# Second attention: an exponential left as two bf16 tiles that TensorE adds

## The chip, the cores and the metric

The kernel runs on one core of a Trainium2 chip. The metric is the device time of one execution in microseconds (us), lower is better. Engines: TensorE (PE) multiplies matrices into PSUM, ScalarE (ACT) computes functions, VectorE (DVE) does elementwise work, GpSimd (POOL) hardly takes part here, SyncE (SP) starts nearly all transfers.

## The reference

Four blocks in a row, each added to x: a linear attention A, a softmax attention B, and both again. The change is in the second B:

```python
def _B_ref(x, wqkv, wo):            # x: 1 x 2048 x 1024 after a layernorm, bf16; H = 32 heads, Dh = 32
    qkv = (x @ wqkv).reshape(B, S, 3, H, Dh).transpose(2, 0, 3, 1, 4)
    q, k, v = qkv[0], qkv[1], qkv[2]
    scores = jnp.einsum("bhqd,bhkd->bhqk", q, k) * (Dh ** -0.5)
    p = _softmax(scores, axis=-1)
    o = jnp.einsum("bhqk,bhkd->bhqd", p, v)
    return o.transpose(0, 2, 1, 3).reshape(B, S, D) @ wo

x = x + _A_ref(_layernorm(x), A_wqkv, A_w_phi, A_wo)
x = x + _B_ref(_layernorm(x), B_wqkv, B_wo)
x = x + _A_ref(_layernorm(x), A_wqkv, A_w_phi, A_wo)
x = x + _B_ref(_layernorm(x), B_wqkv, B_wo)
```

Nothing is subtracted from the scores before the exponential; numerator and denominator come from the same exponentials.

## The kernel before

**The planner.** The program is not written in the order in which it runs. Each step is an entry with an engine, an estimated duration, the steps it needs, the buffers it holds and a priority. On the host, `Sched.run` plays these entries through in estimated time (line 183 on) and so fixes the order on every engine. The chip then runs these fixed orders, held together by semaphores. An estimate that changes can therefore change the order. Estimates that matter here: an activation of n elements n/1200 + 0.064 us; a VectorE step of n elements n/960 + 0.15, and half of the per-element part for a `tensor_scalar` from SBUF to SBUF; one accumulation step of four matmuls 0.225.

**The attention.** There are 32 turns per attention (4 chunks of 512 queries by 8 groups of four heads). A turn has two passes, and each pass 8 blocks of 128 keys with 4 units: 64 units a turn, 2048 in an attention. A unit is one score tile of 128 keys by 512 queries for one head. `score` (L1082) writes it to PSUM with a 32-row matmul. A group of three units goes to ACT as one exponential of 1536 columns (L1139), in two PSUM areas by turns (banks 0 to 2 and 3 to 5). The accumulation (L1264) takes two units in one step: four matmuls of 32 columns each, for each unit one with the values and one with ones, so that numerator and denominator grow together in bank 6.

**The second path.** Some units go past ACT. `spare` picks one that stands 36 to 44 units ahead in the list. It comes either as a fourth score in bank 7 (`attach`, when that bank is free) or in place of the third of a group, whose exponential then has 1024 columns (at most once in some four groups, `MIX`). Two such units make a pair. `convert` (L1221) adds an offset to each score tile in PSUM and leaves it as an integer in one of two `work` slots ("xy"): read as a float, it has the power of two in its exponent bits and the fraction in its mantissa. When the pair is full, `exp_dve` runs five steps over both units (1024 columns): mantissa with exponent zero into the slot "xx", of which there is one (L1048); exponent alone, in place (L1051); and three multiply-adds (all recorded at L1046) that multiply the factors of a polynomial by the power of two and leave a bf16 tile E1 in the arena. A new pair is opened only if a slot of each kind, a turn's allowance (`MOST`) and little waiting work on DVE (`LOAD`) allow it.

**Around it.** PE also runs the projections that later turns and the output need, through bank 7 (L507). Where PE was busy less than 75% of the last 3.4 us, the planner adds filler matmuls: on `onesD` (recorded at L507) or on `zero` (L1490). The two attentions have the same code; the second runs from about 1558 to 2388 us. The arena is 162 KB per partition and handed out by the planner; an E1 tile holds 2 KB, and six may live.

Of the kernel before, what the change touches and what calls it, by code (L numbers as in the profile page):

```python
# [11 lines left out]
ALU = mybir.AluOpType  # L12
AX = mybir.AxisListType
BF16 = mybir.dt.bfloat16
F32 = mybir.dt.float32
I32 = mybir.dt.int32

EPS_LN = 1e-5
EPS_DEN = 1e-6
DH = 32  # L20
C512 = 512
# [316 lines left out]
MIX = (lambda i: 4, lambda i: 3)  # L338
# [20 lines left out]
def kernel(  # L359
# [644 lines left out]
    def b_last(c, t, fc, prio, w, oT, banks, eng, part=None, lo=0, hi=4):  # L1004
# [22 lines left out]
        else:  # L1027
# [2 lines left out]
        dma(prio, lambda: nc.sync.dma_start(  # L1030
            out=out[0, xs, fc * C512:(fc + 1) * C512], in_=r_v()), [e], [r_b], kb=128)

    def exp_dve(pair, prio):


        n = len(pair["got"])
        y_b, e_b = pair["bufs"]
        x_b, x = fixed("xx", [(10,)])
        sch.enter(x_b, prio)
        y_v, x_v, e_v = (lambda v=v: v()[:, 0:n, :] for v in (pair["y"], x, pair["e"]))  # L1040

        def ts(fn, deps, bufs):
            return sch.later("DVE", n * 512 / 1920 + 0.15, fn, deps, bufs, prio)

        def stt(out_, in0, scalar, in1, dep, bufs):
            return sch.later("DVE", dve_us(n * 512), lambda: nc.vector.scalar_tensor_tensor(  # L1046
                out=out_(), in0=in0(), scalar=scalar, in1=in1(), op0=ALU.add, op1=ALU.mult), [dep], bufs, prio)
        m = ts(lambda: nc.vector.tensor_scalar(  # L1048
            out=x_v().bitcast(I32), in0=y_v().bitcast(I32), scalar1=0x007FFFFF, scalar2=0x3F800000,
            op0=ALU.bitwise_and, op1=ALU.bitwise_or), pair["got"], [y_b, x_b])  # L1050
        a = ts(lambda: nc.vector.tensor_scalar(  # L1051
            out=y_v().bitcast(I32), in0=y_v().bitcast(I32), scalar1=0x7F800000, scalar2=None,
            op0=ALU.bitwise_and), [m], [y_b])
# [4 lines left out]
    def attention(base, kT, vT, q_of, gate, most, mix, turns, pos):  # L1058


        units = [
# [93 lines left out]
        def close(pair):  # L1155
            if pair is not None:
                last = pair["units"][0]
                eo = exp_dve(pair, prio_of(last) - LEAD)
                for b in pair["bufs"]:
                    b.left -= 1  # L1160
                for k, u in enumerate(pair["units"]):
                    used(u, eo, pair["bufs"][1], pair["flat"], k)
                state["pair"] = None

        def wants(prio):
# [19 lines left out]
        def spare(rows, turn, more):  # L1185

            pair = state["pair"]
            if state["at"] + AHEAD + 8 > len(units) or (pair is None and (state["turn"].get(turn, 0) + 2 > most(turn) or sch.load("DVE") > LOAD)):
                return None
            u = next((u for u in units[state["at"] + AHEAD:state["at"] + AHEAD + 8]  # L1190
                      if u[4] in rows and u not in taken
                      and all(d.done == 2 for d in needs(u))), None)
            if u is None:
                return None
            new = list(more)
            if pair is None:
                y_b, y_v = fixed("xy", [(8,), (9,)])
                e_b, e_v = sb("E1", 2, C512)
                new += [y_b, e_b]
            for b in new:  # L1200
                sch.enter(b, prio_of(u) - LEAD)
            if not sch._alloc(new):
                for b in new:
                    sch.queue[b.cls][0].remove(b)
                return None
            if pair is None:
                state["pair"] = {"got": [], "units": [], "y": y_v, "e": e_v, "bufs": (y_b, e_b),
                                 "flat": lambda: e_v().rearrange("p a b -> p (a b)")}
                for b in (y_b, e_b):
                    b.left += 1  # L1210
            taken.add(u)
            return u

        def convert(so, u, s_b, s_v, turn):

            pair = state["pair"]
            y_b, y_v = pair["bufs"][0], pair["y"]
            k = len(pair["got"])
            so.bufs += holds(u)
            pair["units"].append(u)  # L1220
            pair["got"].append(sch.later("DVE", dve_us(512), lambda: nc.vector.tensor_scalar(  # L1221
                out=y_v().bitcast(I32)[:, k, :], in0=s_v(), scalar1=EXP2_OFF * ONE, scalar2=0.0,
                op0=ALU.add, op1=ALU.max), [so], [s_b, y_b], prio_of(u) - LEAD, None, True))
            state["turn"][turn] = state["turn"].get(turn, 0) + 1
            if k:
                close(pair)
# [16 lines left out]
        if True:  # L1243
            for qc, g in turns:
                T = []
                end = (qc, g) == turns[-1]
                for pp in range(2):
                    a_b, a_v = ps("acc", [(6,)])
                    last = None
                    for d in range(8):  # L1250
                        prio = base + 10 * pos[(qc, g)] + 5 * pp + 0.5 * d
                        for u in range(2):
                            us = [(qc, g, pp, d, 2 * u + k) for k in range(2)]
                            kc = 4 * (d // 2) + 2 * u + d % 2
                            v_b, v_v, v_done = vT[(g // 4, kc // 4)]

                            def fn(us=us, kc=kc, u=u, d=d, a_v=a_v, v_v=v_v, g=g, pp=pp):
                                for k in range(2):
                                    eb, ev, x = e_of[us[k]]
                                    j = 2 * pp + k  # L1260
                                    for what in range(2):
                                        col = 64 * ((pp + what) % 2) + 32 * k
                                        o = (g % 4) * P + j * DH
                                        nc.tensor.matmul(  # L1264
                                            out=a_v()[col:col + 32, :],
                                            lhsT=v_v()[:, kc % 4, o:o + DH] if what == 0 else ones_bf[:],
                                            rhs=ev()[:, x * C512:(x + 1) * C512],
                                            start=(d == 0 and u == 0), stop=(d == 7 and u == 1),
                                            tile_position=(0, col), skip_group_check=True)
# [81 lines left out]
    for layer in range(2):  # L1351
# [70 lines left out]
        for g in range(G):  # L1422
            pr = at + 10 * pos[(0, g)]
            w = slab("w2", pr - 11, B_w[:, :, g * P:(g + 1) * P], P) if g else wq0
            for qc in range(NC):
# [8 lines left out]
        oTs = attention(at, kT, vT, q_of, gate, MOST[layer], MIX[layer], turns, pos)  # L1434
# [91 lines left out]
```

## Time and profile before

| What | before |
|---|---|
| median of 3 runs | 2403.58 us (2401.06 to 2406.6) |
| profiled execution, its own time | 2402.28 us |
| its span, first to last instruction | 2400.5 us |
| mean granted TensorE clock | 0.993 |
| units converted by DVE, whole program (L1221) | 302 |

The span is the profile's; the time of an execution has 1.8 us around it. PE is TensorE's matmuls, PEld its weight loads, and "busy" of PE includes the modelled tail of each matmul. In a group of instructions the figures behind the bar are the busy time in us and the mean duration of one in ns, then the engine's idle time in front of the group and what ended it. A wait is written "waiting engine and line <- what ended the wait: us in total, times, longest".

### The profile page before, as it was taken

What the parts mean: (1) busy time and instruction counts of PE and PEld (TensorE: products, weight loads), DVE (VectorE), ACT (ScalarE), POOL (GpSimd) and SP (SyncE); (2) the same over time, 40 slices, a digit from 0 to 9 for tenths busy, and PEclk for the clock granted to TensorE, in tenths of its full rate; (3) what the DMA queues carried; (4) which work ended last, traced back from release to release, by engine and by line L of the source; (5) the groups of instructions that cost most, each with busy time, mean ns of one, the idle gap of its engine ahead of it and who ended that gap; (6) DMA issues with size and microseconds to landing.
All of it is one profiled execution on the core that took longest, in us unless ns stands there. A gap on an engine that the chain in (4) does not pass through costs nothing.

```text
span 2400.5 us, 61762 instructions
## 1 busy us (share of the span) xinstructions
PE 2248.0 (94%) x26839; PEld 864.3 (36%) x26904; DVE 1861.2 (78%) x2540; ACT 2042.4 (85%) x1893; POOL 28.0 (1%) x72
## 2 busy tenths in 40 slices
PE   7999999999999998999998999899999999999998
PEld 4443443333333333333333444333333333333333
DVE  6997763565668788987996776456699999998997
ACT  6325657999999999999997456499999999999998
POOL 0000000000000000000000000000000000000000
PEclk9999999999999999999999999899999999999999
DMA  9020010112222221113314100000111111021110
GB/s 220 14 75 1 5 36 17 41 37 48 51 59 73 82 59 55 54 48 110 117 36 143 36 5 25 18 24 26 37 30 41 33 31 33 25 61 42 42 31 28
DMA packets 205192, 117.03 MB, mean 49 GB/s; under 512 B 125304, under 2 KB 194936, under 8 KB 204152
## 3 DMA queue, kind: packets, MB, share of 16 engines
q1 hardware_dynamic: 203864, 110.98, 17.1%
q8 instruction: 210, 3.44, 0.6%
q10 hardware_dynamic: 1056, 2.10, 0.3%
q14 instruction: 62, 0.51, 0.1%
HBM read 77.40 MB, written 15.19 MB: 39 GB/s over the span
## 4 chain that ended last, share of the span: by engine, by line
ACT 35%; PE 13%; issue 9%; DVE 4%; DMA 1%; ACTq 0%; SPq 0%; DVEq 0%
ACT arena L1139 33%; PE psum L503 6%; PE psum L507 2%; PE psum L1082 2%; PE psum L1264 1%; DVE arena L598 1%; ACT arena L696 1%; DVE arena L594 0%; DMA arena<-rd 0%; PE psum L872 0%; DMA arena<-arena 0%; DVE arena L700 0%; PE psum L817 0%; DVE work L1046 0%; DVE arena L709 0%
## 5 line engine op out<-in xcount | busy, mean ns | idle before, releaser
L1139 ACT ACTIVATE arena<-psum 128x1536 bf16<-128x1536 f32 (+1 forms) x1338 | 1712.4, 1553 | 43.0 <-PE psum L1082 38.6
L1264 PE MATMUL psum<-arena 128*32 128x512 bf16 x4096 | 621.1, 383 | 1.5 <-DVE arena L1279 1.4
L1264 PE MATMUL psum<-arena,ones_bf 128*32 128x512 bf16 x4096 | 621.3, 383 | 0.0
L507 PE MATMUL psum<-arena 128*32 128x512 bf16 (+1 forms) x8768 | 607.4, 377 | 12.4 <-DVE xT L1001 2.9
L1082 PE MATMUL psum<-arena 32*128 32x512 bf16 x4096 | 526.5, 383 | 79.2 <-ACT arena L1139 72.7
L503 PE MATMUL psum<-arena 128*128 128x512 bf16 (+1 forms) x1976 | 457.8, 377 | 24.6 <-DVE arena L598 6.0
L1082 PEld LDWEIGHTS <-arena 32*128 32x128 bf16 x4096 | 178.1, 91 | 605.0 <-issue 594.3
L1046 DVE SCALAR_TENSOR_TENSOR work<-work 128x1024 f32<-128x1024 f32 (+1 forms) x310 | 369.4, 1191 | 6.0
L507 PEld LDWEIGHTS <-arena 128*32 128x32 bf16 x8768 | 195.7, 95 | 258.3 <-issue 153.3
L503 PEld LDWEIGHTS <-arena 128*128 128x128 bf16 x2032 | 194.0, 99 | 259.2 <-issue 54.8
L1221 DVE TENSOR_SCALAR work<-psum 128x512 int32<-128x512 f32 x302 | 207.6, 687 | 93.9 <-PE psum L1082 91.2
L1264 PEld LDWEIGHTS <-arena 128*32 128x32 bf16 x4096 | 169.9, 95 | 210.4 <-issue 149.0
L1046 DVE SCALAR_TENSOR_TENSOR arena<-work 128x1024 bf16<-128x1024 f32 (+1 forms) x155 | 184.5, 1190 | 2.6
L1264 PEld LDWEIGHTS <-ones_bf 128*32 128x32 bf16 x4096 | 168.5, 95 | 29.1 <-issue 3.6
L931 DVE CAST arena<-psum 128x512 bf16<-128x512 f32 (+1 forms) x128 | 83.6, 653 | 110.4 <-PE psum L507 110.2
L696 ACT ACTIVATE arena<-psum 128x512 bf16<-128x512 f32 x80 | 42.8, 599 | 85.2 <-PE psum L503 53.8
L1051 DVE TENSOR_SCALAR work<-work 128x1024 int32<-128x1024 int32 (+1 forms) x155 | 104.7, 676 | 3.9
L1048 DVE TENSOR_SCALAR work<-work 128x1024 int32<-128x1024 int32 (+1 forms) x155 | 104.3, 673 | 3.6
L834 ACT ACTIVATE arena<-psum 128x512 bf16<-128x512 f32 x128 | 69.8, 597 | 40.9 <-PE psum L503 32.4
L594 DVE TENSOR_TENSOR arena<-xT,arena 128x1024 f32<-128x1024 bf16 x64 | 78.0, 1220 | 32.3 <-ACT arena L581 32.2
L1279 DVE COPY arena<-psum 128x512 f32<-128x512 f32 x126 | 86.3, 685 | 14.2 <-PE psum L1264 13.2
L507 PE MATMUL psum<-xT,onesD 128*32 128x512 bf16 x1200 | 91.3, 380 | 1.5 <-DVE arena L931 0.6
(97 smaller groups left out, 1387.6 us busy)
## 6 DMA issues: line engine op xcount, KB each, us to landing
arena<-rd SPq DMA_DIRECT2D x62, 256.0 KB
arena<-in_A_wqkv_dram SPq DMA_DIRECT2D x10, 1024.0 KB
arena<-in_B_wqkv_dram SPq DMA_DIRECT2D x35, 256.0 KB
arena<-arena SPq DMA_DIRECT2D x256, 32.0 KB
arena<-in_B_wo_dram SPq DMA_DIRECT2D x32, 256.0 KB
arena<-wd_k SPq DMA_DIRECT2D x8, 1024.0 KB
arena<-arena SPq DMA_DIRECT2D x80, 64.0 KB
arena<-in_A_wo_dram SPq DMA_DIRECT2D x4, 1024.0 KB
```

Of the source, the lines that this page charges most:

```text
L503: nc.tensor.matmul(out_, lhsT=lhsT, rhs=rhs, start=start, stop=stop, skip_group_check=True)
L507: nc.tensor.matmul(out_[ks, :], lhsT=lhsT[:, ks], rhs=rhs, start=start, stop=stop, tile_position=(0, 32 * k), skip_group_check=True)
L594: s1 = op("DVE", dve_us(1024), lambda pr=pr, w_v=w_v: nc.vector.tensor_tensor(out=w_v(), in0=xT[:, pr, csl(c)], in1=m_v().unsqueeze(1).to_ ...
L931: return soon(op("DVE", dve_us(n), lambda: nc.vector.tensor_copy(out=dst(), in_=src()), [dep], bufs, prio))
L1046: return sch.later("DVE", dve_us(n * 512), lambda: nc.vector.scalar_tensor_tensor(out=out_(), in0=in0(), scalar=scalar, in1=in1(), op0=ALU ...
L1048: m = ts(lambda: nc.vector.tensor_scalar(out=x_v().bitcast(I32), in0=y_v().bitcast(I32), scalar1=0x007FFFFF, scalar2=0x3F800000, op0=ALU.b ...
L1051: a = ts(lambda: nc.vector.tensor_scalar(out=y_v().bitcast(I32), in0=y_v().bitcast(I32), scalar1=0x7F800000, scalar2=None, op0=ALU.bitwise ...
L1082: nc.tensor.matmul(out=out_, lhsT=kT[g][1]()[r, pp, d * P:(d + 1) * P], rhs=q_of[(qc, g)][1]()[r, (pp + j // 2) % 2, :], start=True, stop= ...
L1139: ex = make("ACT", act_us(w * C512), lambda: nc.scalar.activation(out=e_v()[:, 0:w * C512], in_=s_v()[:, 0:w * C512], func=ACT.Exp, scale= ...
L1221: pair["got"].append(sch.later("DVE", dve_us(512), lambda: nc.vector.tensor_scalar(out=y_v().bitcast(I32)[:, k, :], in0=s_v(), scalar1=EXP ...
L1264: nc.tensor.matmul(out=a_v()[col:col + 32, :], lhsT=v_v()[:, kc % 4, o:o + DH] if what == 0 else ones_bf[:], rhs=ev()[:, x * C512:(x + 1) ...
L1279: cp = op("DVE", dve_us(512), lambda t_v=t_v, a_v=a_v: nc.vector.tensor_copy(out=t_v(), in_=a_v()), [last], [a_b, t_b], prio - 4)
```

## The change

In the second attention alone (`SPLIT = (False, True)`), a pair's exponential is left as a sum of two bf16 tiles. The first is again polynomial times power of two. The second is the power of two times a fixed 7-bit mantissa (0x39), made exactly by masking the high half of the integer and setting these mantissa bits. PE adds the two when it accumulates. With the constant term taken out, the polynomial needs two multiply-adds where it needed three:

| step | before, 1024 columns | after |
|---|---|---|
| 1 | mantissa to xx, int32 | the same, other exponent bits |
| 2 | exponent alone, int32, in place in xy | exponent and fixed mantissa, uint16, every second half-word of xy into the second half of E1 |
| 3 | (xx + R) * xy into xy | gone |
| 4 | (xx + B) * xx into xx | (xx + B') * xx into xx |
| 5 | (xx + C) * xy into E1, bf16 | (xx + C') * xy into the first half of E1, bf16 |

The tile E1 has room for four tiles of 512 columns in place of two. In the accumulation each converted unit brings two more matmuls, which come behind the four of its step; the planner's estimate of that step grows by 0.2165 us, once per step.

```diff
+EXP2S_OFF = 125.32242318458253
+EXP2S_B, EXP2S_C = -0.05462324649185644, 1.5306572635884585
+EXP2S_D = 0x0039
+SPLIT = (False, True)
...
+    def high(v):
+        return v.bitcast(U16).rearrange("p a (b t) -> p a b t", t=2)[:, :, :, 1]
...
+        if pair["split"]:
+            e2_v = lambda: pair["e"]()[:, 2:2 + n, :]
+            m = ts(lambda: nc.vector.tensor_scalar(
+                out=x_v().bitcast(I32), in0=y_v().bitcast(I32), scalar1=0x007FFFFF, scalar2=0x3F000000,
+                op0=ALU.bitwise_and, op1=ALU.bitwise_or), pair["got"], [y_b, x_b])
+            a = ts(lambda: nc.vector.tensor_scalar(
+                out=e2_v().bitcast(U16), in0=high(y_v()), scalar1=0x7F80, scalar2=EXP2S_D,
+                op0=ALU.bitwise_and, op1=ALU.bitwise_or), [m], [y_b, e_b])
+            h = stt(x_v, x_v, EXP2S_B, x_v, a, [x_b])
+            return stt(e_v, x_v, EXP2S_C, y_v, h, [x_b, y_b, e_b])
...
-        def used(u, ex, e_b, e_v, x):
-            e_of[u] = (e_b, e_v, x)
+        def used(u, ex, e_b, e_v, x, xs=None):
+            e_of[u] = (e_b, e_v, (x,) if xs is None else (x, xs))
             av = av_of[u]
+            if xs is not None:
+                if not any(len(e_of[o][2]) > 1 for o in units[index[u] - u[4] % 2:index[u] - u[4] % 2 + 2] if o != u and o in e_of):
+                    av.dur += 0.2165
...
-                e_b, e_v = sb("E1", 2, C512)
+                e_b, e_v = sb("E1", 4 if split else 2, C512)
...
-                                for k in range(2):
-                                    eb, ev, x = e_of[us[k]]
-                                    j = 2 * pp + k
-                                    for what in range(2):
+                                for n in range(2):
+                                    for k in range(2):
+                                        eb, ev, xs = e_of[us[k]]
+                                        if n >= len(xs):
+                                            continue
+                                        x = xs[n]
+                                        j = 2 * pp + k
+                                        for what in range(2):
...
+                                                start=(d == 0 and u == 0 and n == 0),
+                                                stop=(d == 7 and u == 1 and n == len(xs) - 1),
```

More of the change, by code (lines that the diff above doesn't have):

```diff
@@ L16 @@
 I32 = mybir.dt.int32
+U16 = mybir.dt.uint16
 EPS_LN = 1e-5
@@ L1056, in exp_dve, with attention @@
         return stt(e_v, x_v, EXP2_C, y_v, h, [x_b, y_b, e_b])
-    def attention(base, kT, vT, q_of, gate, most, mix, turns, pos):
+    def attention(base, kT, vT, q_of, gate, most, mix, turns, pos, split):
         units = [
@@ L1161, in close @@
                 for k, u in enumerate(pair["units"]):
-                    used(u, eo, pair["bufs"][1], pair["flat"], k)
+                    used(u, eo, pair["bufs"][1], pair["flat"], k, 2 + k if split else None)
                 state["pair"] = None
@@ L1206, in spare @@
             if pair is None:
-                state["pair"] = {"got": [], "units": [], "y": y_v, "e": e_v, "bufs": (y_b, e_b),
+                state["pair"] = {"split": split, "got": [], "units": [], "y": y_v, "e": e_v, "bufs": (y_b, e_b),
                                  "flat": lambda: e_v().rearrange("p a b -> p (a b)")}
@@ L1221, in convert @@
             pair["got"].append(sch.later("DVE", dve_us(512), lambda: nc.vector.tensor_scalar(
-                out=y_v().bitcast(I32)[:, k, :], in0=s_v(), scalar1=EXP2_OFF * ONE, scalar2=0.0,
+                out=y_v().bitcast(I32)[:, k, :], in0=s_v(), scalar1=(EXP2S_OFF if split else EXP2_OFF) * ONE, scalar2=0.0,
                 op0=ALU.add, op1=ALU.max), [so], [s_b, y_b], prio_of(u) - LEAD, None, True))
@@ L1257, in fn @@
                             def fn(us=us, kc=kc, u=u, d=d, a_v=a_v, v_v=v_v, g=g, pp=pp):
-                                for k in range(2):
-                                    eb, ev, x = e_of[us[k]]
-                                    j = 2 * pp + k
-                                    for what in range(2):
[L1262 to L1269, printed above, removed]
+                                for n in range(2):
[6 more added lines that the diff above has]
+                                        for what in range(2):
+                                            col = 64 * ((pp + what) % 2) + 32 * k
+                                            o = (g % 4) * P + j * DH
+                                            nc.tensor.matmul(
+                                                out=a_v()[col:col + 32, :],
+                                                lhsT=v_v()[:, kc % 4, o:o + DH] if what == 0 else ones_bf[:],
+                                                rhs=ev()[:, x * C512:(x + 1) * C512],
+                                                start=(d == 0 and u == 0 and n == 0),
+                                                stop=(d == 7 and u == 1 and n == len(xs) - 1),
+                                                tile_position=(0, col), skip_group_check=True)
                             last = op("PE", 0.225, fn, flat([last, v_done[(kc % 4, g % 4 // 2)]]),
@@ L1433 @@
                     q_of[(qc, g)] = q_back(g, qc, at + 10 * pos[(qc, g)] - 12, away)
-        oTs = attention(at, kT, vT, q_of, gate, MOST[layer], MIX[layer], turns, pos)
+        oTs = attention(at, kT, vT, q_of, gate, MOST[layer], MIX[layer], turns, pos, SPLIT[layer])
         if last:
```

## The prediction

> **What bounds the kernel now.** I read the page's totals first, then the stages of the second attention (1558 to 2388 us, the only part that the diff reaches), then the instructions and waits inside them.
>
> ```profile
> span 2400.5 us, 61762 instructions
> PE 2248.0 (94%) x26839; PEld 864.3 (36%) x26904; DVE 1861.2 (78%) x2540; ACT 2042.4 (85%) x1893; POOL 28.0 (1%) x72
> ```
>
> By these shares PE would be the limit. The stages say otherwise (columns: stretch and length, then busy us and instructions of each engine, PE clock, DMA share and GB/s):
>
> ```profile
> 1600.00:1800.00 200.00, 196.04 (x2910) 71.53 (x2902) 142.90 (x199) 199.40 (x159) 0.00 (x0) 1.00 0.12 30
> 1800.00:2300.00 500.00, 467.64 (x6692) 164.56 (x6689) 467.97 (x587) 499.95 (x396) 0.00 (x0) 1.00 0.14 39
> 2300.00:2365.00 65.00, 60.94 (x880) 21.87 (x877) 62.20 (x78) 65.00 (x52) 0.00 (x0) 1.00 0.07 21
> ```
>
> ACT (fourth pair) is busy 499.95 of 500 us, so the stage lasts as long as ACT's exponentials do. The chain of waits over 1800 to 2300 agrees, and the groups by shape of that stage show who does what:
>
> ```profile
> by line: ACT arena L1139 77.1%; issue 18.9%; PE psum L1264 1.4%; PE psum L507 1.3%; PE psum L1082 1.2%; ACTq L1139 0.2%; PE psum L1490 0.1%
> ```
>
> ```profile
> L1139 ACT ACTIVATE arena<-psum 128x1536 bf16<-128x1536 f32 x324 | 457.1, 1639 | 0.1
> ...
> L1046 DVE SCALAR_TENSOR_TENSOR work<-work 128x1024 f32<-128x1024 f32 x124 | 151.3, 1220 | 2.4
> ...
> L1139 ACT ACTIVATE arena<-psum 128x1024 bf16<-128x1024 f32 x72 | 88.5, 1229 | 0.0
> L1221 DVE TENSOR_SCALAR work<-psum 128x512 int32<-128x512 f32 x124 | 85.2, 687 | 15.7 <-PE psum L1082 14.2
> ...
> L1046 DVE SCALAR_TENSOR_TENSOR arena<-work 128x1024 bf16<-128x1024 f32 x63 | 76.6, 1216 | 1.1
> ...
> L507 PE MATMUL psum<-xT,onesD 128*32 128x512 bf16 x560 | 44.4, 380 | 1.3 <-DVE arena L931 0.6 <-DVE arena L943 0.5
> L1048 DVE TENSOR_SCALAR work<-work 128x1024 int32<-128x1024 int32 x62 | 42.7, 689 | 1.6
> L1051 DVE TENSOR_SCALAR work<-work 128x1024 int32<-128x1024 int32 x62 | 42.6, 687 | 1.4
> ...
> L1490 PE MATMUL psum<-xT,zero 128*32 128x512 bf16 x276 | 21.8, 379 | 0.0
> ```
>
> A unit is one 128x512 tile of scores. ACT does 324x3 + 72x2 = 1116 units here, at 500/1116 = 0.448 us each (the mean ns of L1139 overlap their neighbours and can't be added). DVE takes the other 124 (L1221), in 62 pairs. It gets no more because it is itself full: 467.97 of 500 us, of which the exponential has 85.2 + 151.3 + 76.6 + 42.7 + 42.6 = 398.4, or 6.43 us a pair, and other work 69.6. By the code a pair needs one of two `work` slots, and the one `xx` slot from its first mask to its last multiply-add, so a new pair starts when DVE has got through an old one. Hence a faster exponential on DVE means more units there and fewer on ACT, which sets the end.
>
> PE has two kinds of room: it waits for ACT, and what it runs on onesD and zero in this attention is filler that the planner puts in when PE was busy under 75% of the last 3.4 us.
>
> ```profile
> PE psum L1082 <- ACT arena L1139: 29.3, 102, 0.9
> DVE work L1221 <- PE psum L1082: 14.2, 34, 1.7
> ```
>
> **The change part by part.** *One multiply-add goes* (the first of the two `work<-work` per pair at L1046): 1.22 us, so a pair costs 6.43 - 1.22 = 5.21 us. The planner's list has the same step out, so the order it writes changes with it.
>
> *The exponent mask becomes a 16-bit one* that reads every second half-word of y and writes packed half-words. No row has a strided read. The nearest is the instruction it replaces, L1051: same engine, operation, count and memory. From 1024 to 512 elements that goes from 687 to 420 ns:
>
> ```profile
> L1051 DVE TENSOR_SCALAR work<-work 128x512 int32<-128x512 int32 x8 | 3.4, 420 | 0.2
> ```
>
> That is 0.53 us for 1024 elements and 0.15 fixed. Below, twice that rate would make 0.15 + 0.27 = 0.42 us; above, the 1.22 us that L1046 takes for as many. I take 0.69, unchanged. The low end brings nothing here, because the host plans this step at 0.68 us and fixes the order; the high end is a rival.
>
> [...]
>
> *More units move.* Let T be the new length of what now takes 500 us, with 1240 units in it, and let DVE keep its busy share of 93.6%. DVE then takes 2 x (0.936 T - 69.6)/5.21 = 0.359 T - 26.7 units; ACT takes the rest, and (1240 - 0.359 T + 26.7) x 0.448 = T. So T = 488.8: 149 units on DVE instead of 124, **11.2 us less**. If DVE could fill every gap, (T - 69.6) in place of (0.936 T - 69.6), T = 484.2 and 15.8 less; if other limits hold the units at 124, nothing.
>
> From 2300 to 2365 DVE is as full (62.2 of 65), and in proportion 65/500 x 11.2 = **1.5 us less**, with 17 units now:
>
> ```profile
> 2300.00:2365.00 65.00, 11.44 (x17) 1.00 0.07 21
> ```
>
> From 1600 to 1800 DVE is busy only 142.90 of 200 us, and stands waiting for PE:
>
> ```profile
> DVE arena L931 <- PE psum L507: 31.0, 17, 3.8
> ...
> DVE work L1221 <- PE psum L1082: 15.3, 14, 2.0
> ...
> PE psum L1082 <- ACT arena L1139: 2.5, 8, 0.5
> ```
>
> A shorter chain gives nothing there; at most a fifth more of its 33 units, 7 x 0.448 = 3.1 us. I take nothing.
>
> *PE adds the second tile*: per unit two more matmuls (values and ones), 32 columns each, behind the four of its step. The starts of steps in one run show the price (first of four of each step):
>
> ```profile
> 1901.72 0.38 PE L1264 MATMUL psum<-arena 128*32 128x512 bf16 x1
> ...
> 1901.94 0.38 PE L1264 MATMUL psum<-arena 128*32 128x512 bf16 x1
> ...
> 1902.15 0.38 PE L1264 MATMUL psum<-arena 128*32 128x512 bf16 x1
> ```
>
> They accumulate into the same bank 0.215 us apart, and the new pieces keep the tiling, so 0.215 us per unit; two units of one step share it. Below, a piece that fills only half the columns may let the next step's other half in beside it, and cost nothing; above, 0.38 if it waited for the whole of the matmul in front. From 1800 to 2300: 149 x 0.215 = 32 us, plus the 11 us that go, against (560 + 276)/4 = 209 fillers x 0.215 = 45 us and the 29.3 us of waits. It is covered, with some 31 us left. From 1600 to 1800 the cover is thin:
>
> ```profile
> L1221 DVE TENSOR_SCALAR work<-psum 128x512 int32<-128x512 f32 x33 | 22.7, 688 | 15.6 <-PE psum L1082 15.3
> ...
> L1490 PE MATMUL psum<-xT,zero 128*32 128x512 bf16 x36 | 3.0, 379 | 0.0
> ...
> L507 PE MATMUL psum<-xT,onesD 128*32 128x512 bf16 x12 | 0.8, 382 | 0.0
> ```
>
> 33 x 0.215 = 7.1 us against 12 fillers x 0.215 = 2.6 and the 2.5 us of waits: 2.0 us short. What is late then are the projections that PE runs between score groups. Their own evacuations wait longer, but ACT idled only 0.6 us in this stage for all reasons, so they run ahead of need and I take nothing. At 0.38 a piece it would be 12.5 - 5.1 = 7.4 us on ACT.
>
> *The tile E1 doubles* from 2 to 4 KB a partition. No view shows the arena's room. A unit is taken 36 to 44 units ahead of the list, about 16 us at 1240/500 = 2.48 units a us, and pairs come every 8.1 us, so two to three such tiles live at once: some 6 KB of 162. I take nothing; the bounds are nothing and the rival's price. No DMA, queue or wait is added, and no step of the first 1558 us is touched.
>
> **Sum.** 11.2 + 1.5 = 12.7 us off the profiled execution's 2402.28 (span 2400.5 and 1.8 around it): 2389.6. The median of the runs lies 1.3 above that execution, so **2391**. With the ends of the unit count: 15.8 + 2.1 (65/500 of it) + 3.1 = 21.0 gives 2383, none gives 2404.
>
> **Rivals.** *The strided mask runs at L1046's rate* (the other side). The order is planned for 0.68 us, so 1.22 makes DVE late by 0.53 us on each of some 84 pairs (149 + 20 units), 45 us from 1800 to 2365. DVE can give up what it now waits for scores, 14.2 us and in proportion 1.8 beyond; the rest of its idle time are gaps between instructions. So 29 us of lateness reach PE's accumulation, then the score banks and ACT: 2391 + 29 = 2420, and 2436 with no slack at all. It loses the gain when the mask takes 0.69 + (16 + 12.7)/84 = 1.03 us. For it: no row shows a 4-byte step at full rate. Against: L1051 takes whole 4-byte words from the same addresses at 0.53 ns each.
>
> *PE takes the brake's place*: with 0.38 us a piece the early stage loses 7.4 us, and 2398 is left. For it: 196 of 200 us busy there. Against: steps 0.215 apart on one bank.
>
> *The units don't move* (it doesn't do what it says): DVE only gets idle, 2404. For it: from 1600 to 1800 DVE has time and takes only 33 units in 200 us, so bank 7 and the spacing of mixed groups limit as well. Against: from 1800 on it takes 124 in 500, a rate half as high again, while DVE is full.
>
> *E1 finds no room*: if a quarter of the attention's 177 units went back to ACT, 44 x 0.448 = 20 us more than now, 2423.
>
> ```profile
> L1221 DVE TENSOR_SCALAR work<-psum 128x512 int32<-128x512 f32 x177 | 121.6, 687 | 34.8 <-PE psum L1082 32.9
> ```
>
> **Chances.** Forecast 0.56 (its own range 2383 to 2397), PE's brake 0.14, units that don't move 0.12, the slow mask 0.12, no room 0.06. A measurement here can tell 0.2%, 4.8 us. The forecast and most of PE's brake make faster 0.68; units that don't move and the rest of it, same 0.15; the last two, with a little from elsewhere, slower 0.17. The range reaches from 2381, just past the upper bound of the gain, to 2411, where it takes in a mask of up to 0.69 + (16 + 20)/84 = 1.12 us.
>
> **What would show it.** Right: no second `work<-work` multiply-add per pair, a 16-bit mask near 0.69 us, some 205 conversions (177 + 25 + 3) in the second attention in place of 177, ACT still without gaps, fewer fillers, first 1558 us as before. Wrong: a mask over 1.0 us with ACT waiting for scores; as many conversions as now and DVE below 85%; PE waiting for nothing while ACT waits for PE; or fewer conversions, which points at the arena.

## The result, and the profile after

The changed kernel takes 2398.53 us, median of 22 runs, against 2401.82 for the kernel before on the same chips, also 22: 3.3 us less. The ratio is 0.9984, with a 95% interval from 0.9977 to 0.9991, that is 2 to 5.5 us. The prediction was 12.7 us. Nearly all of the gain that was forecast came about on ScalarE's exponentials, and most of it was lost again elsewhere.

The page's first line, then the three stages of the second attention (columns as before):

```profile
span 2396.8 us, 61508 instructions
```

```profile
1600.00:1800.00 200.00, 194.47 (x2865) 72.44 (x2865) 128.07 (x190) 194.60 (x154) 0.00 (x0) 1.00 0.12 31
1800.00:2300.00 500.00, 475.73 (x6593) 165.66 (x6594) 445.49 (x597) 495.93 (x395) 0.00 (x0) 1.00 0.14 38
2300.00:2365.00 65.00, 62.24 (x898) 22.40 (x894) 57.85 (x78) 65.00 (x53) 0.00 (x0) 1.00 0.08 25
```

ACT, idle for 0.6 and 0.05 us in the first two stages before, now idles 5.4 and 4.1. DVE has fallen from 467.97 to 445.49 us although it converts more. The groups of 1800 to 2300 us, in which L1160 is now the exponential on ACT, L1242 the conversion, L1054 the multiply-adds and L1061 the new mask:

```profile
L1160 ACT ACTIVATE arena<-psum 128x1536 bf16<-128x1536 f32 x313 | 443.1, 1597 | 3.9 <-PE psum L1289 2.0 <-PE psum L512 0.8 <-PE psum L1100 0.5
...
L1242 DVE TENSOR_SCALAR work<-psum 128x512 int32<-128x512 f32 x148 | 101.6, 687 | 30.3 <-PE psum L1100 29.1 <-issue 0.2
L1160 ACT ACTIVATE arena<-psum 128x1024 bf16<-128x1024 f32 x82 | 97.5, 1188 | 0.2 <-DMA out_dram<-arena 0.2
L1054 DVE SCALAR_TENSOR_TENSOR work<-work 128x1024 f32<-128x1024 f32 x74 | 89.8, 1214 | 0.0
L1054 DVE SCALAR_TENSOR_TENSOR arena<-work 128x1024 bf16<-128x1024 f32 x74 | 89.6, 1211 | 0.8
...
L1061 DVE TENSOR_SCALAR arena<-work 128x1024 uint16<-128x1024 uint16 x74 | 50.7, 686 | 0.1
...
L512 PE MATMUL psum<-xT,onesD 128*32 128x512 bf16 x360 | 29.2, 381 | 1.8 <-DVE work L1242 1.6 <-DVE arena L936 0.2
...
L1516 PE MATMUL psum<-xT,zero 128*32 128x512 bf16 x124 | 10.9, 380 | 0.0
```

One multiply-add per pair is gone, the mask takes 686 ns, 148 units come where 124 came, and PE's fillers fall from 209 to (360 + 124)/4 = 121. Over the whole second attention there are 205 units, from 177:

```profile
L1242 DVE TENSOR_SCALAR work<-psum 128x512 int32<-128x512 f32 x205 | 140.6, 687 | 59.0 <-PE psum L1100 57.7 <-issue 0.2
```

Where the gain went is best seen on ACT alone. The planner counts n/1200 + 0.064 us for an exponential of n columns, 1.344 us for 1536 and 0.917 for 1024. From one start to the next the median in the trace is 1.331 and 0.905 us before, 1.330 and 0.904 after, but summed over the long run of exponentials the planner's figure comes within 0.3 of the 829.7 us that they took before. With this sum as their own time, from the start of the long run (1558.5 us before, 1554.8 after; eight earlier ones stand between other work) to the last, the rest of the time between is what was lost between them:

| | first to last exponential | their own time | lost | last one to the end |
|---|---|---|---|---|
| before | 829.7 | 829.4 | 0.3 | 12.3 |
| after | 828.1 | 817.1 | 11.0 | 13.9 |

The 28 units take 12.3 us off ACT, and 11.0 us are lost in waits and 1.6 in the tail. (With the medians in place of the planner's figure the units take 12.9 us, and after loses 11.3 us more than before in place of 10.7. Records of successive exponentials overlap, 1.60 us each by the row of 1536 columns above and 1.33 from start to start, so the idle times of the rows, 9.5 us, come out a little below the 11.0.) The wait rows of ACT, first for 1600 to 1800 us, then for 2000 to 2100, then for the tail:

```profile
ACT arena L1160 <- PE psum L1100: 5.3, 2, 3.4
```

```profile
ACT arena L1160 <- PE psum L1289: 2.0, 4, 0.9
ACT arena L1160 <- PE psum L512: 0.8, 1, 0.8
ACT arena L1160 <- PE psum L1100: 0.2, 1, 0.2
```

```profile
ACT arena L1322 <- PE psum L1289: 1.8, 1, 1.8
```

The first row is two waits for scores (L1100). The second group is of another kind: an accumulation (L1289) or a projection (L512) makes nothing that an exponential reads, so ACT waited there for the place in the arena that it writes. The last is the end's accumulation, which took 0.5 us of waiting before.

By these two executions alone the attention and its tail gained nothing (842.0 us both), and the 3.7 us between their spans lie ahead of the attention, where the clock of TensorE was lower in the profile of before, 0.93 against 1.00 from 1500 to 1600 us. Whether the clock makes up all of the 3.7 us was not separated (PE clock is the third column from the end; before, then after):

```profile
1500.00:1600.00 100.00, 90.03 (x983) 37.90 (x984) 49.16 (x67) 68.56 (x68) 0.00 (x0) 0.93 0.09 21
```

```profile
1500.00:1600.00 100.00, 89.63 (x1040) 38.09 (x1042) 49.46 (x67) 73.69 (x73) 0.00 (x0) 1.00 0.09 21
```

The 3.3 us come from the medians, not from this pair; which stage holds them is not shown.

How the first stage's waits arise is in its timeline (start, length, engine and line), just ahead of the longer of the two:

```profile
1709.57 0.69 DVE L948 TENSOR_SCALAR arena<-psum 128x512 bf16<-128x512 f32 x1 [5.11 <-PE psum L512]
...
1710.29 0.51 SPq L953 DMA_DIRECT2D arena<-arena  x1
...
1710.85 0.59 SPq L954 DMA_DIRECT2D arena<-arena  x1
...
1713.95 0.61 PE L1100 MATMUL psum<-arena 32*128 32x512 bf16 x6
1714.38 1.45 ACT L1160 ACTIVATE arena<-psum 128x1536 bf16<-128x1536 f32 x1 [3.38 <-PE psum L1100]
```

DVE stands 5.11 us for a query projection of PE, takes it out (L948), SP issues the two copies that swap its halves, and 3.1 us after the second was issued the next scores run, six in a row. Of these 3.1 us PE was idle for 0.64 us, for bank 7 to be emptied, and else busy with accumulations and other projections. The queries were late.

### The profile page after: what moved, and what is told of

Read it like the earlier page. It is cut to its first block, busy times and chain, and to the rows that moved or that the text cites. A ratio compares the mean times of both kernels' runs of the same rounds, so it can differ in the third digit from the quotient of the medians.

```text
span 2396.8 us, 61508 instructions
## 1 busy us (share of the span) xinstructions
PE 2252.0 (94%) x26717; PEld 866.7 (36%) x26782; DVE 1813.6 (76%) x2533; ACT 2031.8 (85%) x1887; POOL 28.4 (1%) x72
## 4 chain that ended last, share of the span: by engine, by line
ACT 28%; PE 17%; DVE 7%; issue 7%; DMA 2%; SPq 0%; ACTq 0%; DVEq 0%
ACT arena L1160 27%; PE psum L508 6%; PE psum L512 4%; PE psum L1100 3%; PE psum L1289 3%; DMA arena<-rd 1%; DVE work L1242 1%; DMA arena<-arena 1%; DVE work L1054 1%; DVE arena L603 1%; DVE arena L1346 1%; ACT arena L701 0%; DVE arena L599 0%; DVE arena L1054 0%; DVE arena L705 0%
## 5 line engine op out<-in xcount | busy, mean ns | idle before, releaser
L1160 ACT ACTIVATE arena<-psum 128x1536 bf16<-128x1536 f32 (+1 forms) x1332 | 1702.5, 1532 | 51.3 <-PE psum L1100 43.8
L1289 PE MATMUL psum<-arena 128*32 128x512 bf16 x4301 | 663.5, 383 | 2.9 <-DVE arena L1305 2.6
L1289 PE MATMUL psum<-arena,ones_bf 128*32 128x512 bf16 x4301 | 663.5, 384 | 0.0
L512 PE MATMUL psum<-arena 128*32 128x512 bf16 (+1 forms) x8768 | 614.5, 378 | 14.1 <-DVE arena L1001 4.0
L1100 PE MATMUL psum<-arena 32*128 32x512 bf16 x4096 | 523.2, 383 | 69.6 <-ACT arena L1160 61.2
L1100 PEld LDWEIGHTS <-arena 32*128 32x128 bf16 x4096 | 173.5, 91 | 592.6 <-issue 581.4
L1242 DVE TENSOR_SCALAR work<-psum 128x512 int32<-128x512 f32 x330 | 226.5, 687 | 119.8 <-PE psum L1100 117.8
L512 PEld LDWEIGHTS <-arena 128*32 128x32 bf16 x8768 | 198.6, 95 | 260.7 <-issue 156.8
L1054 DVE SCALAR_TENSOR_TENSOR work<-work 128x1024 f32<-128x1024 f32 (+1 forms) x233 | 277.5, 1191 | 2.6
L1289 PEld LDWEIGHTS <-arena 128*32 128x32 bf16 x4301 | 189.5, 95 | 224.3 <-issue 145.4
L1054 DVE SCALAR_TENSOR_TENSOR arena<-work 128x1024 bf16<-128x1024 f32 (+1 forms) x169 | 200.9, 1189 | 2.4
L1289 PEld LDWEIGHTS <-ones_bf 128*32 128x32 bf16 x4301 | 187.6, 95 | 33.7 <-issue 5.4
L1346 DVE TENSOR_TENSOR arena<-arena 64x512 bf16<-64x512 f32 x124 | 84.7, 683 | 17.8 <-DMA arena<-rd 15.9
L564 ACT ACTIVATE arena<-xT 128x2048 bf16<-128x2048 bf16 (+1 forms) x28 | 49.7, 1794 | 42.7 <-DVE xT L912 17.8
L603 DVE TENSOR_TENSOR arena<-arena 128x1024 bf16<-128x1024 f32 x64 | 77.4, 1223 | 10.4 <-ACT arena L593 9.1
```

Of the source, the lines that this page charges most:

```text
L512: nc.tensor.matmul(out_[ks, :], lhsT=lhsT[:, ks], rhs=rhs, start=start, stop=stop, tile_position=(0, 32 * k), skip_group_check=True)
L603: fin.append(op("DVE", dve_us(1024), lambda pr=pr, w_v=w_v: nc.vector.tensor_tensor(out=xv()[:, pr, :], in0=w_v(), in1=r_v().unsqueeze(1). ...
L1100: nc.tensor.matmul(out=out_, lhsT=kT[g][1]()[r, pp, d * P:(d + 1) * P], rhs=q_of[(qc, g)][1]()[r, (pp + j // 2) % 2, :], start=True, stop= ...
L1160: ex = make("ACT", act_us(w * C512), lambda: nc.scalar.activation(out=e_v()[:, 0:w * C512], in_=s_v()[:, 0:w * C512], func=ACT.Exp, scale= ...
L1289: nc.tensor.matmul(out=a_v()[col:col + 32, :], lhsT=v_v()[:, kc % 4, o:o + DH] if what == 0 else ones_bf[:], rhs=ev()[:, x * C512:(x + 1) ...
L1346: s = [op("DVE", dve_us(512), lambda a=a, k=k, o_v=o_v, r_v=r_v, T=T: nc.vector.tensor_tensor(out=o_v()[a, :], in0=T[k][1]()[a, :], in1=r_ ...
```

## The experiments

The theory formed from this profile: DVE's gain is real, and it is lost at two places, early because PE has no room for the added matmuls there, late because the larger tile fills the arena. The rivals: the moved units are worth less than thought; or the added matmuls slow PE all along. In the table, idle is ACT's idle time from 1600 to 1800 us, and own time, lost and units are as above.

| run | idle early | own time | lost | units | median, us | ratio to before (95%) |
|---|---|---|---|---|---|---|
| before | 0.6 | 829.4 | 0.3 | 177 | 2401.82 | |
| after | 5.4 | 817.1 | 11.0 | 205 | 2398.53 | 0.9984 (0.9977 to 0.9991) |
| 1 DVE alone | 1.5 | 818.0 | 1.4 | 204 | 2390.74 | 0.9952 (0.9939 to 0.9964) |
| 2 DVE and tile | 1.6 | 817.5 | 1.4 | 204 | 2393.35 | 0.9961 (0.9946 to 0.9976) |
| 3 DVE and PE | 5.5 | 819.0 | 6.5 | 202 | 2397.35 | 0.9982 (0.9971 to 0.9994) |
| 4 from turn 7 | 0.6 | 818.4 | 8.2 | 203 | 2397.15 | 0.9978 (0.9965 to 0.9990) |
| 5 both removed | 0.2 | 819.8 | 1.7 | 200 | 2392.38 | 0.9972 (0.9960 to 0.9983) |
| 6 two small tiles | 0.5 | 821.1 | 0.0 | 196 | 2390.30 | 0.9963 (0.9950 to 0.9975) |
| 7 old steps, PE doubled | 1.4 | 829.8 | 3.9 | 177 | 2403.06 | 1.0012 (1.0000 to 1.0024) |
| 8 a gap in the turns | 0.3 | 820.2 | 1.7 | 198 | 2393.25 | 0.9972 (0.9955 to 0.9988) |
| 9 queries earlier | 5.2 | 819.3 | 8.6 | 200 | 2398.80 | 1.0003 (0.9991 to 1.0015) |
| 10 early turns kept | 5.0 | 820.6 | 5.4 | 197 | 2397.63 | 0.9984 (0.9970 to 0.9998) |
| 11 no bank 7 early | 0.9 | 822.0 | 3.6 | 195 | 2394.51 | 0.9976 (0.9962 to 0.9989) |

The kernel before had medians from 2400.04 to 2401.82 beside them. The runs were measured on several chips, each with the kernel before beside it, so two rows are best set against each other by their ratios. By these, runs 1, 2 and 6 are clearly faster than the changed kernel and run 7 is slower; run 9's interval touches that of the changed kernel, those of runs 3, 4, 5, 8, 10 and 11 overlap it, and for them the idle and lost times, from one profile each, carry more than the medians do.

**1, 2 and 3: the parts apart.** Run 1 keeps the shorter chain and takes both prices away, run 2 brings back the tile, run 3 the matmuls.

```diff
 # runs 1 and 3
-            e2_v = lambda: pair["e"]()[:, 2:2 + n, :]
+            e2_v = lambda: pair["e"]()[:, 0:n, :]
-                e_b, e_v = sb("E1", 4 if split else 2, C512)
+                e_b, e_v = sb("E1", 2, C512)
...
 # runs 1 and 2
-                    used(u, eo, pair["bufs"][1], pair["flat"], k, 2 + k if split else None)
+                    used(u, eo, pair["bufs"][1], pair["flat"], k)
 # run 3
+                    used(u, eo, pair["bufs"][1], pair["flat"], k, k if split else None)
```

> Leaves out: the second bf16 tile is written where the last step writes over it, E1 stays at 2 KB and PE adds nothing; the shorter DVE chain is all that is left of the change. Theory (the gain is real and is spent elsewhere, about 6 us on an early PE without room and 3 to 4 us on the arena): some 205 conversions in the second attention, no gaps on ACT over 1 us between 1600 and 2365 us, and 11 to 13 us faster than before (ratio about 0.995). Rival (moved units are worth less than 0.448 us each, or the planner loses the gain by itself): about as many conversions, but no more than 5 us faster (0.998).

> Leaves out: the second tile is made and has its 4 KB in the arena, but PE does not add it. Arena theory: E1 at twice the size keeps ACT's own tiles out of the arena for a while between 2000 and 2080 us; the kernel loses 2 to 4 us of the first run's gain there, and ACT shows waits on L1289, none between 1650 and 1725. Early-PE theory alone: as fast as the first run.

> Leaves out: E1 stays at 2 KB, and PE adds the first tile twice in place of the second; PE's work is that of the change. Early-PE theory: ACT stands 5 to 7 us between 1650 and 1725 us, waiting for scores whose projections are late, and hardly elsewhere; 5 to 7 us behind the first run. Rival (the added pieces slow PE all along the attention): ACT's waits are spread over all stretches from 1800 on, more than 1 us in each 100 us. Arena theory alone: as fast as the first run.

Run 1 is 10.0 us faster than before with 204 units, a little under the 11 to 13 expected; one wait of 1.5 us near 1709 us is left where none over 1 us was expected. So the units are worth what they should be, and the shorter chain does its part. The stages of run 1 (two), and then the early stage of run 3:

```profile
1600.00:1800.00 200.00, 193.73 (x2894) 71.17 (x2886) 136.06 (x195) 198.46 (x157) 0.00 (x0) 1.00 0.12 31
1800.00:2300.00 500.00, 468.13 (x6645) 164.69 (x6638) 443.22 (x593) 499.70 (x401) 0.00 (x0) 1.00 0.14 39
```

```profile
1600.00:1800.00 200.00, 194.68 (x2866) 72.52 (x2859) 124.23 (x185) 194.50 (x154) 0.00 (x0) 1.00 0.12 31
```

Run 3 has the early waits of the changed kernel and no others to speak of; of its 6.6 us behind run 1, 5.1 are lost between the exponentials and 1.0 is their own time, with two units fewer on DVE. That PE is slowed all along has fallen. The stretch from 2000 to 2100 us in the changed kernel, in run 2 and in run 3:

```profile
2000.00:2100.00 100.00, 94.43 (x1269) 32.23 (x1270) 89.48 (x120) 96.70 (x76) 0.00 (x0) 0.98 0.10 27
```

```profile
2000.00:2100.00 100.00, 91.87 (x1262) 31.86 (x1262) 91.70 (x122) 100.00 (x80) 0.00 (x0) 1.00 0.11 27
```

```profile
2000.00:2100.00 100.00, 92.50 (x1223) 31.13 (x1215) 92.14 (x124) 100.00 (x81) 0.00 (x0) 1.00 0.11 29
```

The expectation for run 2 missed: the tile alone costs ACT nothing between 2000 and 2100 us, nor do the matmuls alone. Only both together do: 3.3 us of idle time. (By its median run 2 is 2.6 us behind run 1, as the expectation had it, but with six executions of each and nothing more lost between the exponentials; 1.3 us of it are a longer tail in this profile.) Run 3 and the changed kernel have the same work on PE and differ in the size of the tile, so the size is needed for it; but it takes PE's added work as well. By the code a step of the accumulation holds its tiles until it is done, so later steps keep tiles longer; no run takes that link alone; the plan shows it (below).

**4, 5 and 8: where the pairs keep the old steps.** Run 4 leaves turns 0 to 6 as before; run 5 does so too and has the small tile of run 3; run 8 leaves turns 0 to 6, 18 and 19, with the real tile.

```diff
-                e_b, e_v = sb("E1", 4 if split else 2, C512)
+                e_b, e_v = sb("E1", 4 if split and turn >= SPLIT_FROM else 2, C512)
-                state["pair"] = {"split": split, "got": [], ...
+                state["pair"] = {"split": split and turn >= SPLIT_FROM, "got": [], ...
...
 # run 8: (7 <= turn < 18 or turn >= 20) in place of turn >= SPLIT_FROM, which is 7 in runs 4 and 5
```

> The change, but pairs opened in turns 0 to 6 (up to about 1740 us) keep the old five steps and the small tile. Early-PE theory: no waits of ACT over 1 us between 1600 and 1740, those near 2000 to 2080 stay; 4 to 6 us faster than the changed kernel. Rival (PE slowed all along): no more than 1 us faster than the changed kernel, since only some 30 of 205 units lose their second tile.

> Leaves out: as the run with pairs split from turn 7 on, but E1 keeps 2 KB and PE adds the first tile twice in place of the second. If a late projection in the early stage and a full arena later are all that eats the gain, ACT loses no more than 2.5 us between its exponentials in the second attention, and the kernel is 8 to 10 us faster than before (ratio 0.996). If the added matmuls cost time of their own after turn 7, it stays within 5 us of before (0.998), like the run from turn 7 with the large tile.

> The whole computation: the change with its 4 KB tile, but pairs opened in turns 0 to 6 and in 18 and 19 keep the old five steps and the small tile. By the two causes named, the waits of ACT at 1650 to 1725 and at 2000 to 2075 are gone and no more than 3 us lost in all; 6 to 9 us faster than before. Rival (the arena is full elsewhere too): ACT's waits on accumulations move to other turns, and it is no faster than the changed kernel.

In run 4 the early waits go as expected, but the kernel gains only 1.4 us on the changed one, where 4 to 6 were expected: later losses grow from about 5 to 8 us. Stages of run 4:

```profile
1600.00:1800.00 200.00, 195.67 (x2885) 71.45 (x2885) 140.57 (x199) 199.40 (x158) 0.00 (x0) 1.00 0.12 30
1800.00:2300.00 500.00, 470.57 (x6453) 163.46 (x6445) 441.68 (x590) 495.04 (x394) 0.00 (x0) 1.00 0.14 38
```

Most of its waits are for the accumulation: 5.9 us on L1290 over the whole second attention, against 2.7 on scores. Run 5 differs from it in the tile's size alone (PE adds the first tile twice, which is as much work), and loses 1.7 us in place of 8.2:

```profile
1800.00:2300.00 500.00, 470.23 (x6453) 164.09 (x6447) 441.99 (x590) 498.38 (x399) 0.00 (x0) 1.00 0.14 38
```

It is 8.3 us faster than before, as expected. The medians of runs 4 and 5 lie 4.8 us apart, though the intervals of their ratios overlap. That is the clearest sign in the runs that the tile makes the larger part of the late loss. Run 8 gets there with the real computation, with small tiles in turns 18 and 19, and is 7.4 us faster than before, inside the 6 to 9 expected.

**6: a version that is faster than both.** The second tile gets a place of its own of 2 KB, and pairs of turns 0 to 7 and 17 to 20 keep the old five steps.

```diff
...
+                f_b, f_v = sb("E2", 2, C512) if split and (turn >= 8 and not 17 <= turn < 21) else (None, None)
-            e2_v = lambda: pair["e"]()[:, 2:2 + n, :]
+            e2_v = lambda: pair["e2"]()[:, 0:n, :]
...
```

> The whole computation: the second bf16 tile has a 2 KB place of its own, and pairs opened in turns 0 to 7 and 17 to 20, where PE or the arena has no room, keep the old five steps. By the two causes named: ACT loses no more than 2 us, some 195 conversions, 7 to 10 us faster than before, 4 to 7 faster than the changed kernel. Rival (the gain needs all pairs): some 4 us faster than before, as the changed kernel.

It loses nothing between its exponentials, and with 196 units it is 10.4 us faster than before by the medians, just above the 7 to 10 expected (0.9963, 0.9950 to 0.9975). Each set against the kernel before beside it, it is 5 us (ratios) to 7 us (medians) faster than the changed kernel:

```profile
1600.00:1800.00 200.00, 196.07 (x2899) 71.54 (x2896) 143.87 (x202) 199.46 (x159) 0.00 (x0) 1.00 0.12 30
1800.00:2300.00 500.00, 476.11 (x6645) 165.82 (x6642) 455.97 (x599) 500.00 (x398) 0.00 (x0) 1.00 0.14 38
```

**7, 9, 10 and 11: what the early loss is made of.**

```diff
 # run 7: old five steps and small tile, first tile accumulated twice (as run 3)
 # run 9
-                        q_of[(qc, g)] = b_q(g, qc, pq - 8, wq, FIL)
+                        q_of[(qc, g)] = b_q(g, qc, pq - (14 if last and pos[(qc, g)] < 8 else 8), wq, FIL)
...
 # run 10: as run 8, with (not 17 <= turn < 21)
 # run 11
-            taken7 = sch.bank_used[7]
+            taken7 = sch.bank_used[7] or (split and turn < 7)
```

> Leaves the gain out: the old five steps on DVE and the old tile of 2 KB, but PE adds each converted tile twice, so only PE's added work is left. Early-PE theory: ACT stands 2 to 6 us more than before between 1600 and 1800 us, the kernel is 3 to 7 us slower than before. If PE has the room that the prediction gave it: within 1 us of before.

> The whole computation: the changed kernel, with the query projections of the first eight turns of the second attention 6 earlier in priority. If PE as a whole has no room in the early stage, the two waits of ACT at 1650 and 1700 only move: 5 to 7 us of waits somewhere between 1600 and 1800, and the time of the changed kernel within 2 us. If only these two projections were placed too late, the waits go and the kernel gains 4 to 6 us on the changed one.

> The whole computation: the changed kernel, but pairs opened in turns 17 to 20 keep the old five steps and the small tile, so that the arena has more room when it is fullest; the early turns are left as changed. If the late waits come from the arena: about 6 us of waits between 1650 and 1725 stay, those between 2000 and 2100 fall from 4 to under 1 us, and it is 1 to 4 us faster than the changed kernel. If they come from elsewhere, they stay at 2000 to 2100.

> The whole computation: the changed kernel, but in turns 0 to 6 of the second attention no unit is taken through bank 7, where the projections run; units in place of a group's third stay. If the early waits are PE's capacity alone, ACT idles 4 to 6 us between 1600 and 1800 as in the changed kernel. If the shorter chain on DVE adds to them by taking bank 7 from the projections, ACT's idle time there falls to 1 to 3 us, and the kernel is up to 3 us faster than the changed one.

Run 7 missed downwards: 2.4 us slower than before, where 3 to 7 were expected, and in the early stage only 0.8 us more idle time on ACT than before. The matmuls alone hardly hurt there; nor does the shorter chain alone (run 1, 0.9 more). Together they cost 5. Run 9 makes the queries earlier, and the wait only moves, from 1714 to 1774 us, where one of 5.08 us stands for the two before:

```profile
1774.73 26.18 ACT L1160 ACTIVATE arena<-psum 128x1536 bf16<-128x1536 f32 x21 [5.08 <-PE psum L1100]
```

So it is not the place of these projections in the order but PE's work as a whole that has no room. The median is that of the changed kernel, as expected; by its ratio (1.0003) run 9 gains nothing on before. Run 10 keeps the early waits (5.0 us) and loses the late ones, as the theory has it; its 0.9 us on the changed kernel, where 1 to 4 were expected, can't be told from nothing. Eight units fewer on DVE, 3.5 us of own time, eat most of the 5.6 us that it loses less:

```profile
1600.00:1800.00 200.00, 195.16 (x2871) 72.85 (x2864) 127.80 (x190) 195.01 (x155) 0.00 (x0) 1.00 0.12 31
1800.00:2300.00 500.00, 474.21 (x6602) 165.17 (x6598) 449.61 (x592) 499.74 (x400) 0.00 (x0) 1.00 0.14 38
```

Run 11 suggests why two small costs make a large one. Bank 7 serves both the projections and the extra units. A chain that is over sooner frees a slot sooner, the next unit takes bank 7, and a projection waits. With that path shut in the early turns, ACT idles 0.9 us there in place of 5.4, for 29 units in place of 34; the kernel is 4.0 us faster than the changed one by the medians, 2 by the ratios, whose intervals overlap:

```profile
1600.00:1800.00 200.00, 196.26 (x2882) 72.29 (x2881) 118.80 (x178) 199.10 (x158) 0.00 (x0) 1.00 0.12 30
```

These five units are also 1.1 us less work for PE (0.215 us each), so the run doesn't part the bank from the work wholly. Nor is the bank alone enough: of the units from 1600 to 1800 us those that do not replace the third of a group came through bank 7, some 4 before (33 units, 29 exponentials of 1024 columns), 7 in the changed kernel (34 and 27), none in run 11, but 11 in run 1 (38 and 27), which idles 1.5 us.

**What the plan says.** The order and the buffers are fixed on the host, so `Sched.run` of each kernel can be read for them. Its times are the planner's estimates, not measurements. In the second attention of the changed kernel's plan ACT's exponentials wait 4.7 us for room in the arena, all of it from 2026 to 2080 us; in run 4's plan 4.4 us, in run 11's 3.0, run 9's 2.2, run 2's 1.1, in run 8's and run 10's 0.1, and in those of before and of runs 1, 3, 5, 6 and 7 nothing. When one waits so, mostly four E1 tiles are live, and 2 to 13 KB are free in all, but no piece of the 3 KB that the output of three units takes. So what is missing is one piece of 3 KB, and only plans with the 4 KB tile ever miss it. Run 4's plan has another 4.5 us of waits for the limit of six such outputs (`QUOTA`), run 5's 1.9, run 7's 3.7: this part of the late loss needs no large tile, only accumulations that come late. The plan also has the whole outcome in it: it ends 3.6 us later with the change than without (2409.7 against 2406.1), but at 2397.1 in run 1 and 2399.1 in run 6.

## Why the prediction was wrong, step by step

- *ACT sets the end, and a unit is worth 0.448 us*: right. 28 units took 12.3 us off the exponentials, 0.44 each (12.9 and 0.46 by the measured medians).
- *One multiply-add less lets DVE take more units*: right, and to the count: 205 were forecast, 205 came. Run 1 is the test of it: with nothing else changed, 10.0 of the 12.7 us appear in the time. That the count is exact is luck in part: DVE did not keep its 93.6% (89.1% from 1800 to 2300 us, 88.6% in run 1), and 148 units came in 500 us, where the sum's own rate gives 153.
- *The mask at 0.69 us*: right, 686 ns (L1061). Here the 16-bit mask that reads every second half-word took as long for 1024 elements as the 4-byte mask in its place did (687 ns, L1051 before), and the rival that had it at L1046's 1.22 us is out.
- *0.215 us per added piece*: right for most of them. In the changed kernel four matmuls start together (within 0.01 us), as a slot, each 0.215 us, and a piece of two (1653.01) comes behind; the first two matmuls of the projection that follows start 0.06 us after it, the other two 0.22:

```profile
1652.36 0.38 PE L1289 MATMUL psum<-arena 128*32 128x512 bf16 x1
...
1652.58 0.38 PE L1289 MATMUL psum<-arena 128*32 128x512 bf16 x1
...
1652.79 0.38 PE L1289 MATMUL psum<-arena 128*32 128x512 bf16 x1
...
1653.01 0.38 PE L1289 MATMUL psum<-arena 128*32 128x512 bf16 x1
...
1653.07 1.61 PE L512 MATMUL psum<-arena 128*32 128x512 bf16 x24
```

So the next matmuls can start beside a half-filled slot. But over all stretches of 32-column matmuls between two groups of scores (1560 to 2365 us), the 169 with an odd number of such pieces are half a slot (0.10 us on the mean) longer for their number of matmuls than the other 447: on the average a piece that finds no partner costs its whole 0.215 us, and not the 0.38 of the rival.

- *From 1600 to 1800 us "2.0 us short", "they run ahead of need and I take nothing"*: the step that failed first. The projections there don't run ahead of need: the queries of the next turn arrive just in time, and ACT idled 5.4 us in place of 0.6. The shortfall was read rightly and then priced at nothing, on the ground that ACT had idled only 0.6 us. Idle time says how late things have been, not how much later they may get. And the 2.0 us left out what the change does to the projections besides: units that come sooner take their bank (run 11, as far as it parts the two).
- *E1 at 4 KB, "two to three such tiles live at once", nothing taken*: the step that failed second, with 3 to 5 us (runs 4 and 5 against each other, 6.5 us in another setting, where a part is the limit of six outputs). By the plan mostly four such tiles were live where it counted, not two to three. The rival had pairs sent back to ACT; no pair was lost, 205 came. What found no room was ACT's own output, and it cost ACT time only where PE was late as well.
- *PE takes the brake's place, 2398*: the nearest rival, and its time came out, by luck: its place was right, but its 7.4 us were not made as it says. The pieces cost 0.215 us, not 0.38, the early stage lost some 5 us, and the rest came from the late waits and the tail, which it does not have.
- *The tail*: taken as fixed; it grew by 1.6 us, as the last accumulations came later (1.8 us of waiting in place of 0.5).

## What to carry to other kernels

When the bound engine is relieved, price what the relief adds on every other engine stage by stage, not over the whole: PE had some 31 us to spare from 1800 us on by the prediction's sum, and none in the 200 us ahead of it. Where a stage stands at 98% of an engine, as this one did (PE busy 196.04 of 200 us), a shortfall of 2 us is not free because nothing waits yet: ACT then idled 5.4 us in place of 0.6; look for the transfer that arrives last and how long before its use it arrives. And a larger buffer in a shared arena can strike whoever allocates next, not its own users; giving it in two smaller pieces, and only where there is room, kept the gain here. And where a host plans the order, read its plan first: here its waits for room and its end showed the loss without the chip.

## What the runs showed of the hardware

In the profiles of four kernels the clock of TensorE fell once in the middle of the second attention: in the changed one (mean 0.91 from 2000 to 2020 us, and 0.50 in the 2 us from 2002), and in runs 4 (0.91 from 2175 to 2195), 9 (0.91 from 2000 to 2020) and 11 (0.91 from 1890 to 1910). All four have the added matmuls and late waits of ACT's exponentials for accumulations (2.0, 5.9, 2.4 and 1.0 us); but so has run 7 (2.6 us), whose clock was 1.00 in every 100 us from 1600 to 2300, so these alone don't explain it. The changed kernel in steps of 2 us (time; us; busy time of PE, its weight loads, DVE, ACT and POOL; PE clock third from the end):

```profile
1998.00:2000.00 2.00, 0.87 (x15) 0.30 (x7) 2.00 (x3) 2.00 (x3) 0.00 (x0) 1.00 0.00 0
2000.00:2002.00 2.00, 1.81 (x26) 0.71 (x27) 1.97 (x3) 2.00 (x2) 0.00 (x0) 0.87 0.05 9
2002.00:2004.00 2.00, 2.00 (x23) 0.42 (x15) 1.90 (x3) 1.74 (x2) 0.00 (x0) 0.50 0.01 1
2004.00:2006.00 2.00, 2.00 (x27) 0.64 (x23) 0.16 (x1) 1.49 (x2) 0.00 (x0) 0.77 0.00 0
```

What is missing to a clock of 1, (0.13 + 0.50 + 0.23) times 2 us, is 3.4 us at half; in steps of 0.2 us the clock is below 1 from 2001.4 to 2005.0 us. Ahead of it, from 1998 to 2000 us, PE is idle for 1.1 us; what set the fall off stays open. How much of the late loss is its doing was not separated: in run 4 ACT idled 2.4 us between 2000 and 2100 us with the clock at full (1.00).
